# Which MLP units of an HGRN2 + GELU kernel are done by blocks and which by block products: two by blocks instead of three

## The chip, the cores and the metric

The kernel runs on one core of a Trainium2 chip. The metric is the device time of one execution in microseconds, of which three runs of the kernel before are given. The engines have the names of the profile: PE is TensorE (PEld its weight loads), DVE is VectorE, ACT is ScalarE, POOL is GpSimd, and SP is the queue that issues DMAs.

## The reference

The first half is a gated linear recurrence (4 batches, 8 heads, 768 tokens, head dimension 48). The second half is an MLP over the 3072 tokens with a model dimension of 384 and an inner dimension of 2048. The inputs q, k, v and f_logit are float32; the two weight matrices arrive as float64.

```python
def _attn_ref(q, k, v, f_logit):
    f = 1.0 / (1.0 + np.exp(-f_logit))
    state = np.zeros((B, H, D, D))
    for t in range(S):
        state = f[:, :, t, :, None] * state + np.einsum('bhd,bhe->bhde', k[:, :, t], v[:, :, t])
        y[:, :, t] = np.einsum('bhd,bhde->bhe', q[:, :, t], state)
    return y

x = attn_out.transpose(0, 2, 1, 3).reshape(B * S, H * D)

def _moe_ref(x, w_in, w_out):
    h = x @ w_in
    g = h * (1.0 / (1.0 + np.exp(-1.702 * h)))
    return g @ w_out
```

## The kernel before

The 3072 tokens are cut into 12 units of 256, three to a batch. Each unit has an attention (the recurrence in chunks: six levels of scores `sc`, a state `st`, an output `y`, which is turned and written to the tile `xT`) and an MLP (`h` = x times w_in, gelu to `g`, `o` = g times w_out). The attention of unit n is emitted in parts, and between the parts the function `merge` emits pieces of the MLPs of earlier units from the list `fill`, so many columns of TensorE work per part. So TensorE runs the MLP of the earlier units inside the attention of unit n. Attention parts on VectorE are the promotes (L519, L523: X times the decays), the evacuations of scores (L466, L485) and the state (L667, L668); on ScalarE the copies Kc and Qc (L494, L500), which stand between two promotes.

An MLP can be done in two ways.

*Plain, by blocks.* `mlp_h` (L1100) does 16 column blocks of w_in with 3 matmuls of 256 columns each, 48 in all; `mlp_o` (L1114) does 32 matmuls of 384 columns. `mlp_block(n, r)` does a quarter r of the inner dimension, so that it needs only that quarter of the weights; its o is added into a sum by VectorE (L1166). A quarter is usable when its weights are converted from float64 bits (L228 on ScalarE, L230 to L233 on VectorE; 16 pairs of blocks in the order in which the quarters need them, three buffers named `bits`, and a new fetch whenever a pair is done). The argument `pieces` of `merge` says how many conversions its parts carry, and `by` how early.

*By block products.* `mlp_h20` replaces h by 20 products of blocks (4 matmuls of 128 columns each, L1006, 80 in all) that use sums of blocks of w_in (names c1 to c4, p1 to p19) and sums of blocks of x (the tiles E, 12 sums on GpSimd, L968); the products are joined into g by VectorE (L1034) and ScalarE (L1013 to L1036). `mlp_o7` replaces o by 7 products (56 matmuls of 192 columns, L869), with four sums of blocks of w_out (T1 to T4, L783, VectorE) and sums of g (L804 to L813). The order of the 20 products is written out in `WHOLE`; its first seven are c3, c1, p7, a21, c2, p15, p9, and p1 is the tenth.

The sums of w_in are made once. Some need new tiles (`sums_of_w`: c3, p15, c2, p6 and later c1, c4, p12, p4, p16). Others overwrite w_in itself (`sums_in_place`), so they may only run once no plain h needs w_in any more: k, p3, p1 and p14 on GpSimd, p7, p19, p9, p5 and p11 on VectorE. p9 overwrites a11, which p3 reads first. Those with a minus sign, such as p4, run on VectorE (L928), the others of `sums_of_w` on GpSimd (L930); p15's second step reads p4.

Before the change, units 0, 1 and 2 are plain by blocks (`N_FILL` = 3). Unit 3 has a plain h and an o by products. Units 4 to 11 have both by products. The first set of sums of w_in is made inside the attention of unit 3, the second set and those of w_out inside that of unit 4.

TensorE and GpSimd run in the order in which the code emits their work. So do VectorE and ScalarE until `fill_order.close()`; after that, a scheduler may put what is emitted later ahead into gaps that it sees. The tile `xT` has three buffers, which the E tiles share: a unit by products needs all three, so two earlier units' plain h must be over before its sums of x begin.

Of the kernel before, what the change touches and what calls it, by code (L numbers as in the profile page):

```python
# [23 lines left out]
def kernel(  # L24
# [33 lines left out]
    nc = tc.nc  # L58
    B, H, S, D = q.shape
    DM = H * D  # L60
# [4 lines left out]
    U = 256  # L65
# [7 lines left out]
    NK = DM // P  # L73
    NFF = DFF // P
    FG = 4
    PAIRS_AHEAD = 3
    N_FILL = 3
    HALF = U // 2
    SLOT = NP * HALF
    NA = NP * U  # L80
# [236 lines left out]
    last = {}  # L317

    def attention(n):
# [265 lines left out]
        def turn_k(a0):  # L585
            if a0 == 0:
                new_kn()
            if n < N_FILL + 1:
                pt = bank([P, 2, 2, P], f"tkn_{n}_{a0}")
            else:  # L590
                pt = ps.tile([P, 2, 2, P], F32, tag="sc", name=f"tkn_{n}_{a0}")
            for a in range(2):
                for f in range(2):
                    x = (a0 + a) * HALF
                    nc.tensor.transpose(pt[:, a, f, :], slot((KR, KF)[f])[:, x:x + HALF], ident)
            nc.scalar.copy(t["kn"][:, a0:a0 + 2], pt)
# [75 lines left out]
        def _():  # L672
# [45 lines left out]
            xTs[n] = xT  # L718
            if n == 0:
                fetch_weights()  # L720
            if n > N_FILL:
                sums_of_x(n)

        def whole(py):
# [181 lines left out]
    def sums_of_w(names):  # L906

        for name in names:
            if name == "p16":
                WA[name] = wp.tile([P, 2 * DM], F32, tag="s", name="N_p16", bufs=1)[:, :FG * P]  # L910
            else:
                WA[name] = const.tile([P, FG * P], F32, name=f"N_{name}")
        first = (
            ("c3", "a30", "", "a32"), ("p15", "a21", "+", "a31"), ("c2", "a11", "+", "a12"), ("p6", "c2", "+", "a22"),
            ("p6", "p6", "", "c3"),
        )
        second = (
            ("c1", "a01", "+", "a02"), ("c4", "a02", "", "a00"), ("p12", "a11", "", "c4"), ("p4", "c1", "-", "a30"),
            ("p12", "p12", "+", "a10"), ("p16", "a20", "", "a21"), ("p12", "p12", "+", "a20"), ("p15", "p15", "", "p4"),
            ("p16", "p16", "", "a22"),  # L920
        )
        for out, x, op, y in first if "c3" in names else second:
            yield lambda x=(out, x, op, y): sum_of_w(nc.vector if x[2] == "-" else nc.gpsimd, *x)

    def sum_of_w(engine, out, x, op, y):
# [6 lines left out]
    def sums_in_place(engine):  # L932

        assert not w_sums
        if engine == nc.gpsimd:
            for out, at in (("p7", "a01"), ("p19", "a12"), ("p5", "a31"), ("p9", "a11"), ("p11", "a00")):
                WA[out] = WA[at]
            sums = (
                ("k", "a02", "a02", "+", "a30"), ("p3", "a02", "a11", "", "k"), ("p1", "a32", "a21", "+", "c3"),
                ("p14", "a10", "a10", "", "c2"),  # L940
            )
        else:
            sums = (
                ("p7", "a01", "a11", "", "c3"), ("p19", "a12", "c2", "-", "a20"), ("p9", "a11", "c4", "", "a11"),
                ("p5", "a31", "a31", "", "c3"), ("p11", "a00", "a00", "", "c1"),
            )
        for out, at, x, op, y in sums:
            WA[out] = WA[at]
            sum_of_w(engine, out, x, op, y)

    def sums_of_x(n):

# [174 lines left out]
    def mlp_unit(n, fill):  # L1127
# [10 lines left out]
        if width(n) > U:  # L1138
            before = fill[-2 * HF:]
            del fill[-2 * HF:]  # L1140
        if n > N_FILL:
            return mlp_h20(n, g, before) + o
        by_block = {}

        def end():

            g[0], g[1] = (by_block["tile", i] for i in range(2))
            sums_of_a(n, g)
            sums_in_place(nc.gpsimd)
            lanes["o"] = [next(turns) % 4 for _ in range(4)]  # L1150
        return mlp_h(n, range(NFF), by_block) + [(0, end, 0)] + o[:HF] + [(0, lambda: sums_in_place(nc.vector), 0)] + o[HF:]

    sums = {}

# [64 lines left out]
    def merge(n, fill, columns, share, pieces=0, hold=0, by=1.0, chores=[], per=3, deal=()):  # L1219
# [10 lines left out]
        for kind, fn in parts:  # L1230
# [15 lines left out]
            def some(end):  # L1246
                nonlocal done
                while fill and done < end and fill[0][2] <= ready:
                    w, emit, _ = fill.pop(0)
                    emit()  # L1250
                    done += w
            jobs = [convert] * n_ops + chores[:per]
            del chores[:per]
            for i, job in enumerate(jobs):
                some(first + n_columns * i / len(jobs))
                job()
# [13 lines left out]
    def opening():  # L1270
# [44 lines left out]
        for _ in range(NOP):  # L1315
            convert()

    fill = []
    opening()
    fill += mlp_blocks((0, 0)) + mlp_blocks((0, 1))  # L1320
    merge(1, fill, UNIT // 2 - LAG // 2 - 3 * DM, steady, 13, hold=1)
    fill += mlp_blocks((1, 0), (1, 1)) + mlp_blocks((0, 2), (1, 2))
    merge(2, fill, UNIT + 3 * DM, steady, 12)
    fill += mlp_blocks((2, 0), (2, 1)) + mlp_blocks((2, 2), (0, 3)) + mlp_blocks((1, 3), (2, 3))
    w_sums = [*sums_of_w(("c3", "p15", "c2", "p6"))]
    merge(3, fill, 3 * UNIT // 2 - LAG // 2, steady, 5, by=0.7, chores=w_sums, per=1)
    fill_order.close()
    for n in range(N_FILL, NALL):
        fill += mlp_unit(n, fill)
    with nc.allow_non_contiguous_dma("one token"):  # L1330
        for h in range(2):
            nc.sync.dma_start(out=q_end[h * HS:h * HS + D], in_=q[B - 1, h::2, S - 1, :].rearrange("a d -> d a"))
    assert not w_sums
# [38 lines left out]
```

## Time and profile before

| what | value |
|---|---|
| three runs, median (lowest to highest) | 599.36 us (598.73 to 599.51) |
| the profiled execution, first to last instruction | 594.5 us |
| TensorE clock granted over the span | 0.994 of full speed |
| DMA, mean over the span | 98 GB/s |
| plain h, L1100, records and busy time | 384, 89.6 us |
| plain o, L1114 | 192, 65.5 us |
| o by products, L869, TensorE share of the last chain by tile (Y, Z, X, W) | 11%, 8%, 4%, 4% |
| sums of w_in in place on GpSimd begin, after a wait for TensorE's last plain h | 224.3 us |
| first sum of x for a unit by products (unit 4) | 242.5 us |

A line of a timeline reads: start and duration in us, engine, line of the kernel, operation, output and inputs by name, shapes, and how many records were merged into the line; in square brackets stands the time for which the engine was idle before it and what ended the wait. A matmul of float32 leaves two records. A line of a table by stretch has the stretch, its length, the busy time of each engine with its number of records, the clock, and the DMA share and rate.

### The profile page before, as it was taken

What the parts mean: (1) busy time and instruction counts of PE and PEld (TensorE: products, weight loads), DVE (VectorE), ACT (ScalarE), POOL (GpSimd) and SP (SyncE); (2) the same over time, 40 slices, a digit from 0 to 9 for tenths busy, and PEclk for the clock granted to TensorE, in tenths of its full rate; (3) what the DMA queues carried; (4) which work ended last, traced back from release to release, by engine and by line L of the source; (5) the groups of instructions that cost most, each with busy time, mean ns of one, the idle gap of its engine ahead of it and who ended that gap; (6) DMA issues with size and microseconds to landing.
All of it is one profiled execution on the core that took longest, in us unless ns stands there. A gap on an engine that the chain in (4) does not pass through costs nothing.

```text
span 594.5 us, 18457 instructions
## 1 busy us (share of the span) xinstructions
PE 574.9 (97%) x7814; PEld 513.6 (86%) x7814; DVE 429.5 (72%) x696; ACT 291.9 (49%) x613; POOL 138.4 (23%) x214
## 2 busy tenths in 40 slices
PE   6879899999999999999999999999999999999997
PEld 6756776867768789999999999999999999999897
DVE  2898987964866858789778778786887786462284
ACT  4746643453334353474474474573663564452440
POOL 4031200230027216610610700800700602203000
PEclk9979999999999999999999999999999999999999
DMA  7947859840243552353552343553361211001000
GB/s 181 215 124 179 193 145 225 217 100 1 52 106 66 145 130 65 80 139 77 127 146 51 84 113 91 130 134 60 88 168 44 63 38 29 28 3 27 28 1 27
DMA packets 82834, 58.29 MB, mean 98 GB/s; under 512 B 33153, under 2 KB 74785, under 8 KB 82753
## 3 DMA queue, kind: packets, MB, share of 16 engines
q1 hardware_dynamic: 82416, 56.73, 38.9%
q8 instruction: 61, 1.00, 0.7%
q10 hardware_dynamic: 337, 0.39, 0.3%
q14 instruction: 20, 0.16, 0.1%
HBM read 43.98 MB, written 8.39 MB: 88 GB/s over the span
## 4 chain that ended last, share of the span: by engine, by line
PE 87%; DVE 7%; ACT 3%; issue 1%; DMA 1%; POOL 1%; SPq 0%; DVEq 0%; ACTq 0%
PE h L1006 17%; PE h L1100 13%; PE o_Y L869 11%; PE o L1114 10%; PE o_Z L869 8%; PE h_y L1006 6%; PE sc L425 6%; PE o_X L869 4%; PE o_W L869 4%; PE y L689 2%; PE t L357 2%; PE y L534 2%; PE sc L643 1%; DVE X L519 1%; ACT yT L703 1%
## 5 line engine op out<-in xcount | busy, mean ns | idle before, releaser
L1100 PE MATMUL h<-xT,w_in 128*128 128x256 f32 x384 | 89.6, 388 | 1.4 <-DMA xT<-yT 1.4
L523 DVE TENSOR_TENSOR X<-X,tot 128x1024 f32<-128x1024 f32 x45 | 57.0, 1266 | 39.8 <-PE sc L425 33.2
L1100 PEld LDWEIGHTS h<-xT,w_in 128*128 128x128 f32 x384 | 72.8, 193 | 13.8 <-DMA xT<-yT 2.4
L494 ACT COPY Kc<-X 128x512 f32<-128x512 f32 x72 | 48.4, 672 | 65.7 <-DVE X L523 51.5
L1114 PE MATMUL o<-w_out,g 128*128 128x384 f32 x192 | 65.5, 491 | 0.4 <-DVE w_out L233 0.4
L968 POOL TENSOR_TENSOR E<-xT 128x128 f32<-128x128 f32 (+1 forms) x32 | 17.9, 571 | 204.0 <-DMA xT<-yT 112.0
L1114 PEld LDWEIGHTS o<-w_out,g 128*128 128x128 f32 x192 | 35.4, 190 | 22.8 <-DVE w_out L233 1.0
L1006 PE MATMUL h<-E,w_in 128*128 128x128 f32 (+1 forms) x420 | 53.4, 275 | 0.0
L869 PE MATMUL o_Y<-T,S 128*128 128x192 f32 x288 | 50.6, 329 | 0.0
L1006 PEld LDWEIGHTS h<-E,w_in 128*128 128x128 f32 x420 | 50.1, 192 | 0.0
L1036 ACT ACTIVATE g<-g 128x512 f32<-128x512 f32 (+1 forms) x63 | 35.6, 584 | 26.0 <-DVE g L1034 25.3
L1104 ACT ACTIVATE g<-h 128x256 f32<-128x256 f32 x64 | 23.8, 382 | 49.0 <-PE h L1100 48.6
L869 PEld LDWEIGHTS o_Y<-T,S 128*128 128x128 f32 x288 | 46.8, 190 | 0.5
L1034 DVE TENSOR_TENSOR g<-g,h 128x512 f32<-128x512 f32 (+1 forms) x52 | 31.8, 632 | 14.3 <-PE h L1006 13.3
L485 DVE COPY_PREDICATED A<-masks,sc 128x256 f32<-128x256 uint32 (+1 forms) x98 | 42.0, 506 | 0.1
L703 ACT COPY yT<-y 48x256 f32<-48x256 f32 x88 | 32.2, 366 | 18.3 <-PE y L689 17.2
L372 POOL TENSOR_SCALAR F<-F 128x1024 f32<-128x1024 f32 x10 | 17.2, 1716 | 95.9 <-ACT F L375 84.3
L345 DVE STREAM_TRANSPOSE X<-raw 128x512 f32<-128x512 f32 x36 | 38.1, 1105 | 0.1
L425 PEld LDWEIGHTS sc<-X,Kc 48*64 48x64 f32 x1440 | 26.2, 136 | 11.1 <-ACT Kc L494 4.8
L425 PE MATMUL sc<-X,Kc 48*64 48x64 f32 x1440 | 31.0, 222 | 4.8 <-ACT Kc L494 1.9
L1034 DVE TENSOR_TENSOR g<-g,h_y 128x512 f32<-128x512 f32 (+1 forms) x26 | 16.5, 634 | 22.3 <-PE h_y L1006 21.4
L1025 ACT ACTIVATE g<-h 128x512 f32<-128x512 f32 (+1 forms) x46 | 26.1, 576 | 10.8 <-PE h L1006 10.6
(162 smaller groups left out, 1156.2 us busy)
## 6 DMA issues: line engine op xcount, KB each, us to landing
bits<-in_moe_w_out_dram SPq DMA_DIRECT2D x8, 768.0 KB, 7.2
raw<-in_f_logit_dram SPq DMA_DIRECT2D x48, 96.0 KB, 3.5
raw<-in_k_dram SPq DMA_DIRECT2D x48, 96.0 KB, 3.0
bits<-in_moe_w_in_dram SPq DMA_DIRECT2D x8, 576.0 KB
raw<-in_q_dram SPq DMA_DIRECT2D x44, 96.0 KB, 2.3
k_tok<-z SPq DMA_DIRECT2D x56, 64.0 KB, 1.8
kt<-k_tok SPq DMA_DIRECT2D x14, 256.0 KB, 2.8
out_dram<-osb SPq DMA_DIRECT2D x18, 192.0 KB, 2.7
```

The lines of the kernel that those rows point to most:

```text
L345: nc.vector.transpose(view(out, at, [[HALF, NP], [step, R4], [R4 * step, 32]]), by_half[:, j, f].rearrange("p a (j d) -> p (a j) d", j=R4) ...
L425: nc.tensor.matmul(t["sc"][h][g * HS:(g + 1) * HS, a, s, :], lhsT=t["Kc", l][rows(h), x:x + HS], rhs=rhs(h, a, g), start=True, stop=True,)
L485: moved = nc.vector.copy_predicated(out=view(A, c * HALF + at, dims), mask=mask.bitcast(U32), data=got)
L494: nc.scalar.copy(c.rearrange("p (n two m) -> p n two m", two=2, m=m), view(X, KF * SLOT, [[2 * m, SLOT // (2 * m)], [(KR - KF) * SLOT + m, ...
L523: nc.vector.tensor_tensor(x, x, y, ALU.mult)
L703: nc.scalar.copy(view(yT[rows(h)], at, [[U, NP], [step, HS]]), py[columns(h, g), g, :, f, :])
L869: nc.tensor.matmul(t[name], lhsT=lhs(f), rhs=rhs(f), start=(new and i == 0), stop=(i == HF - 1), skip_group_check=True,)
L1006: nc.tensor.matmul(ph[:, t], lhsT=WA[a][:, f * P:(f + 1) * P], rhs=E[n][b], start=(root and t == 0), stop=not goes_on, skip_group_check=True,)
L1034: nc.vector.tensor_tensor(to, to, part, ALU.add if sign > 0 else ALU.subtract)
L1036: nc.scalar.activation(to, to, AF.Gelu_apprx_sigmoid)
L1100: nc.tensor.matmul(ph, lhsT=w_in[:, c, ff * P:(ff + 1) * P], rhs=xTs[n][:, c, :], start=(c == 0), stop=(c == NK - 1))
L1114: nc.tensor.matmul(t["po"], lhsT=g[ff // FG][:, ff % FG, tt * P:(tt + 1) * P], rhs=w_out[:, ff, :], start=(ff == ffs[0]), stop=(ff == ffs[ ...
```

## The change

Units 0 and 1 stay plain by blocks. Unit 2 becomes a unit by products whole, and so does unit 3 (its h; its o was already). `merge` for unit 3 now emits the last quarters of units 0 and 1 and then unit 2 by products. All sums of w_in are made inside unit 3's attention: twelve of them as chores of `merge`, whatever is left of them together with unit 2's sums of x and the sums in place after the first o matmul of the last blocks. p9 and the two steps of p16 come after the last o of these blocks, and there the program order of VectorE and ScalarE ends. The eight sums of w_out are put among unit 2's products. Two conversion instructions move from the attention of unit 3 into that of unit 2, and those that stay come earlier in it. `turn_k` of unit 3 uses the bank `sc` for its transposes.

```diff
+    N_BLOCK = 2
...
-            if n < N_FILL + 1:
+            if n < N_FILL:
                 pt = bank([P, 2, 2, P], f"tkn_{n}_{a0}")
...
-            if n > N_FILL:
+            if n >= N_FILL:
                 sums_of_x(n)
...
-            ("p12", "p12", "+", "a10"), ("p16", "a20", "", "a21"), ("p12", "p12", "+", "a20"), ("p15", "p15", "", "p4"),
-            ("p16", "p16", "", "a22"),
+            ("p12", "p12", "+", "a10"), ("p12", "p12", "+", "a20"), ("p15", "p15", "", "p4"),
         )
-        for out, x, op, y in first if "c3" in names else second:
+        last = ("p16", "a20", "", "a21"), ("p16", "p16", "", "a22")
+        for out, x, op, y in {"c3": first, "c1": second, "p16": last}[names[0]]:
...
-        if n > N_FILL:
-            return mlp_h20(n, g, before) + o
-        by_block = {}
-
-        def end():
-
-            g[0], g[1] = (by_block["tile", i] for i in range(2))
-            sums_of_a(n, g)
-            sums_in_place(nc.gpsimd)
-            lanes["o"] = [next(turns) % 4 for _ in range(4)]
-        return mlp_h(n, range(NFF), by_block) + [(0, end, 0)] + o[:HF] + [(0, lambda: sums_in_place(nc.vector), 0)] + o[HF:]
+        return mlp_h20(n, g, before) + o
...
-            jobs = [convert] * n_ops + chores[:per]
-            del chores[:per]
+            jobs = [convert] * n_ops + [lambda: chores and chores.pop(0)()] * per
...
+    def last_blocks():
+
+        hs, os = zip(*(mlp_block(n, NGR - 1) for n in range(N_BLOCK)))
+
+        def sums_left():
+            for x in w_sums:
+                x()
+            w_sums.clear()
+            sums_of_x(N_BLOCK)
+            sums_in_place(nc.gpsimd)
+            last_w.extend(sums_in_place(nc.vector))
+            for x in last_w[:-1]:
+                x()
+            lanes["o"] = [next(turns) % 4 for _ in range(4)]
+
+        def order_ends():
+            last_w[-1]()
+            for x in sums_of_w(("p16",)):
+                x()
+            fill_order.close()
+        o = sum(os, [])
+        return sum(hs, []) + o[:1] + [(0, sums_left, 0)] + o[1:] + [(0, order_ends, 0)]
+
+    def first_whole(n):
+
+        h, of_b = mlp_unit(n, fill), [*sums_of_b()]
+        while of_b:
+            x = of_b.pop()
+            h.insert(2 * len(of_b) + 4, (0, x, 0))
+        return h
...
-    merge(2, fill, UNIT + 3 * DM, steady, 12)
-    fill += mlp_blocks((2, 0), (2, 1)) + mlp_blocks((2, 2), (0, 3)) + mlp_blocks((1, 3), (2, 3))
-    w_sums = [*sums_of_w(("c3", "p15", "c2", "p6"))]
-    merge(3, fill, 3 * UNIT // 2 - LAG // 2, steady, 5, by=0.7, chores=w_sums, per=1)
-    fill_order.close()
+    merge(2, fill, UNIT + 3 * DM, steady, 13)
+    fill += last_blocks() + first_whole(N_BLOCK)
+    w_sums = [*sums_of_w(("c3", "p15", "c2", "p6")), *sums_of_w(("c1", "c4", "p12", "p4"))]
+    last_w = []
+    merge(3, fill, 2 * UNIT + H20 + 7 * HF * HC - LAG - (3 * UNIT // 2 - LAG // 2), steady, 4, by=0.3, chores=w_sums, per=2)
...
-    of_b = [*sums_of_b()]
-    for x in sums_of_w(("c1", "c4", "p12", "p4", "p16")):
-        w_sums += of_b[:1] + [x]
-        del of_b[:1]
-    w_sums += of_b
     for n in range(4, NALL):
-        merge(n, fill, (H20 if n > N_FILL + 1 else NFF * NK * U) + 7 * HF * HC, late, chores=w_sums if n == 4 else [])
+        merge(n, fill, H20 + 7 * HF * HC, late)
```

More of the change, by code (lines that the diff above doesn't have):

```diff
@@ L943, in sums_in_place @@
             sums = (
-                ("p7", "a01", "a11", "", "c3"), ("p19", "a12", "c2", "-", "a20"), ("p9", "a11", "c4", "", "a11"),
-                ("p5", "a31", "a31", "", "c3"), ("p11", "a00", "a00", "", "c1"),
+                ("p7", "a01", "a11", "", "c3"), ("p19", "a12", "c2", "-", "a20"), ("p5", "a31", "a31", "", "c3"),
+                ("p11", "a00", "a00", "", "c1"), ("p9", "a11", "c4", "", "a11"),
             )
@@ L948, in sums_in_place @@
             WA[out] = WA[at]
-            sum_of_w(engine, out, x, op, y)
+            if engine == nc.gpsimd:
+                sum_of_w(engine, out, x, op, y)
+        return [lambda x=(out, x, op, y): sum_of_w(engine, *x) for out, at, x, op, y in sums]
     def sums_of_x(n):
@@ L1332 @@
             nc.sync.dma_start(out=q_end[h * HS:h * HS + D], in_=q[B - 1, h::2, S - 1, :].rearrange("a d -> d a"))
-    assert not w_sums
-    of_b = [*sums_of_b()]
-    for x in sums_of_w(("c1", "c4", "p12", "p4", "p16")):
-        w_sums += of_b[:1] + [x]
-        del of_b[:1]
-    w_sums += of_b
     for n in range(4, NALL):
-        merge(n, fill, (H20 if n > N_FILL + 1 else NFF * NK * U) + 7 * HF * HC, late, chores=w_sums if n == 4 else [])
+        merge(n, fill, H20 + 7 * HF * HC, late)
     for _, emit, _ in fill:
```

## The prediction

> **What bounds the kernel now.** I read the page's busy shares and slices first: TensorE (PE) is full.
>
> ```profile
> PE 574.9 (97%) x7814; PEld 513.6 (86%) x7814; DVE 429.5 (72%) x696; ACT 291.9 (49%) x613; POOL 138.4 (23%) x214
> ...
> PE   6879899999999999999999999999999999999997
> ...
> DVE  2898987964866858789778778786887786462284
> ...
> POOL 4031200230027216610610700800700602203000
> ```
>
> Then the table of waits, TensorE alone, 40 to 240 us. It sums to under 4 us in 200, so TensorE's work sets the end, and work taken off it is time won unless a new wait takes its place.
>
> ```profile
> PE tkn L595 <- DVE X L519: 1.6, 1, 1.6
> PE sc L425 <- DVE st L668: 0.5, 2, 0.3
> PE y L689 <- DVE st L668: 0.5, 1, 0.5
> ```
>
> Then busy time by stretch (columns: PE, PEld, DVE, ACT, POOL). From 124 to 150 us, which the change refills, VectorE (DVE) idles 4.5 and 7.4 us and GpSimd (POOL) nearly throughout. The last row is one steady unit: 43.20 us, all TensorE.
>
> ```profile
> 124.00:137.60 13.60, 13.60 (x124) 9.92 (x117) 9.14 (x12) 5.27 (x12) 0.82 (x1) 1.00 0.22 50
> 137.60:150.30 12.70, 12.70 (x106) 8.72 (x100) 5.28 (x10) 3.83 (x9) 0.00 (x0) 1.00 0.01 1
> ...
> 286.40:329.60 43.20, 43.20 (x657) 42.00 (x658) 32.65 (x52) 23.98 (x47) 11.86 (x19) 1.00 0.45 108
> ```
>
> **What comes off TensorE.** Durations are start to start in the timeline; a matmul leaves two records.
>
> ```profile
> 170.49 5.38 PE L1114 MATMUL o<-w_out,g 128*128 128x384 f32 x16
> 175.71 1.46 PE L1100 MATMUL h<-xT,w_in 128*128 128x256 f32 x6
> ...
> 205.78 18.40 PE L1100 MATMUL h<-xT,w_in 128*128 128x256 f32 x84
> 224.01 2.11 PE L869 MATMUL o_Y<-w_out,g 128*128 128x192 f32 x12
> ...
> 236.70 2.76 PE L869 MATMUL o_Y<-T,S 128*128 128x192 f32 x16
> 239.30 2.76 PE L869 MATMUL o_Z<-T,g 128*128 128x192 f32 x16
> ```
>
> Plain o: 5.22 us for 8, 0.653 each. Plain h: 18.23 for 42, 0.434. o by products: 2.60 for 8, 0.325. h by products (255.04 to 256.82, 16 records): 0.2225. A unit's h falls from 48 x 0.434 = 20.83 to 80 x 0.2225 = 17.80: 3.03 less, for units 2 and 3, 6.06. Unit 2's o falls from 32 x 0.653 = 20.90 to 56 x 0.325 = 18.20: 2.70. Sum: **-8.76 us**. Cross-check: unit 4's attention with unit 3's h took 46.3 us (187.9 to 234.2), a steady unit 43.2; the 3.1 is one unit's h.
>
> **What is added, and hidden.** Units 2 and 3 now each need 12 GpSimd sums of x (0.42 us each) and ten VectorE sums of g (0.69), ScalarE's copies too. The built order of TensorE, VectorE and ScalarE is unchanged over its last 300 rows, and unit 3's is that of a steady unit, which hides all this behind 43.2 us of TensorE: nothing. Unit 2's sums of g stand behind p9 (below) as a steady unit's stand behind its scores. Two conversion instructions move from the third merge into the second (1.9 us of VectorE); its waits of 1.92, 1.23 and 0.38 at 98.7, 101.5 and 107.6 cover them; without these, up to 1.9. The last weight fetch moves ahead on SP's queue, stores of sums give way to stores of osb, and q_end's small load moves back: TensorE waited 0.3 us for DMAs from 40 to 240 us, so nothing. Unit 3's turn_k takes the sc bank, idle then: nothing.
>
> **The new chain.** The last blocks' h come earlier, unit 0's at 130.7 us instead of 159, unit 1's at 137 instead of 176, and unit 2's products follow. VectorE's order up to them is one queue. I lay it on the old clock.
>
> Up to 130.5 us it is the old schedule; two sums for T (1.82) and two F transposes (1.95) fit gaps of 1.58 and 2.16. Then conversion of pair 14 (2.7), three sums (1.4), two for T (1.8): 136.4. TensorE gives scores at 136.5; two promotes with the ScalarE copy between, and evacuation, take 5.45 (138.73 to 144.17 in the old trace): 141.95. Pair 15 (2.8): 144.75. TensorE wants that pair at its third o: 130.7 + 12 h 5.2 + scores 1.1 + 12 h 5.2 + scores 1.1 + two o 1.3 = 144.6. No slack.
>
> Then promote 1.15, evacuation 0.65, N_p4 0.6: 147.15. GpSimd waits for N_p4: p15 1.24, 12 sums of x 5.0, k and p3 2.5: 155.9. VectorE: four in-place sums 2.6, four o sums 1.9, transposes 1.95, three for T 2.75: 156.35, then p9 0.65: 157.0. TensorE's seventh product needs p9: 144.6 + 14 x 0.653 + 6 x 0.89 = 159.1. Slack 2.1. Behind p15 on GpSimd stand all sums of x and in place; behind p9 on VectorE T4's second half and unit 2's sums of g, for which ScalarE's gelus and then unit 2's o wait, all later than the seventh product.
>
> **The price not in that sum.** GpSimd now runs ten weight sums without a break from 120.1, where it ran three, and VectorE works beside it throughout. The timeline shows what happens when both add in SBUF:
>
> ```profile
> 123.54 1.27 POOL L930 TENSOR_TENSOR N_c<-w_in 128x512 f32<-128x512 f32 x1
> ...
> 224.26 3.19 POOL L930 TENSOR_TENSOR w_in<-w_in 128x512 f32<-128x512 f32 x2 [14.39 <-PE h L1100]
> ```
> ```profile
> 120.73 1.72 DVE L523 TENSOR_TENSOR X<-X,F 128x1024 f32<-128x1024 f32 x1 [1.58 <-ACT Qc L500]
> ...
> 138.73 1.23 DVE L523 TENSOR_TENSOR X<-X,tot 128x1024 f32<-128x1024 f32 x1 [3.23 <-PE sc L425]
> ...
> 224.65 1.67 DVE L806 TENSOR_TENSOR g<-g,g 128x512 f32<-128x512 f32 x1
> ...
> 227.49 1.74 DVE L930 TENSOR_TENSOR w_in<-N_c,w_in 128x512 f32<-128x512 f32 x1 [1.17 <-POOL w_in L930]
> ```
>
> Alone, L523 takes 1.23 and a 128x512 sum 0.69. Eight collisions cost VectorE 0.49, 0.80, 0.28 (L523), 1.05, 0.98, 1.05, 1.07 (sums) and 0.40 (L230): mean 0.77. GpSimd loses too (3.19 for two). Transposes and PSUM readers did not lose.
>
> First part, up to pair 15: eleven VectorE instructions on SBUF alone meet those sums, 11 x 0.77 = 8.4 at most. Counting only kinds seen waiting (three L523, two tensor_scalar), 3.8; no collision, 0.15. GpSimd's five small products at 71.8 took 4.03 beside L232 and L233, against 2.07 at 118.1, so the conversions do collide; but some sums will fall into transposes and evacuations. I take six, 4.6. Second part, to p9: GpSimd waits behind four in-place sums (2.6), VectorE in front of T, T, T and p9 (4 x 0.77 = 3.1): 5.7 - 2.1 slack = 3.6 at most; seen kinds only, 2.6 + 0.77 - 2.1 = 1.3; none, 0. I take 1.7, nearer the row. Stall: 6.3, between 0.15 and 12.0. A gain here is excluded: TensorE cannot run before its operands.
>
> The Trainium skill (SBUF — State Buffer, section "SBUF: two separate sides") speaks against this change: it calls the port pair that VectorE and GpSimd share an exclusive lock, held for the whole instruction, against any Vector instruction with two SBUF inputs. By that rule every one of these instructions waits, and the sum would lie at the upper end, near 602.6; by the kinds seen waiting it is 595.7. The waits above (0.28 to 1.07 of a 1.24 us sum) fit a lock met midway.
>
> **Sum.** -8.76 + 6.3 = -2.46 on a span of 594.5, so 592.0. About 4.9 us lie around the span (median 599.36), unchanged: **596.9 us**. From unit 4's first scores on, nothing changes but the clock's offset, so a stall is never won back.
>
> **Rivals.** (1) The cover holds: GpSimd's sums fall into VectorE's transposes and waits, stall 0.15, time 590.8. For it: 124 to 150 us has 12 us of idle VectorE. Against: the queue laid out above fills them. (2) All given back: stall 7.6 to 10.0, 598.2 to 600.6, no change. For it: most of the fifteen collisions at 0.77. (3) Slower: TensorE stands at the seventh product because p9 is last in a chain through both engines (N_p4, p15, twelve sums of x, k, p3, p9). All fifteen collisions: 8.4 + 3.6 = 12.0, time 602.6; it decides from where p9 lands later than 159.1 + 8.76 + 1.2 = 169.1 on the old clock. For it: 3.19 and 1.67 at 224 us show strict turns. Against: it needs every collision. That the change does not do what it says is out: the built order has units 2 and 3 in 80 and 56 products.
>
> **Numbers.** What this kernel's measurement tells from no change is 0.2%, 1.2 us. Forecast (part of the gain kept, 592 to 598): 0.41. Rival 1: 0.17. Rival 2: 0.18. Rival 3: 0.24. Faster 0.58, same 0.18, slower 0.24. Range 591.0 to 602.0: from rival 1 to most of rival 3; the forecast's own is 592 to 598.
>
> **What would show it.** TensorE's plain h records fall from 384 to 192, plain o from 192 to 128. In its waits a new row of some microseconds: the third matmul of the last blocks' o or their scores behind w_out's conversion or X (part one), and an h product behind w_in (p9, part two). GpSimd's ten sums take clearly over 12.4 us from start to end, and N_p4 starts near 151, not 147. If there is no such wait, rival 1 is right; if the wait is on a DMA or on E, the chain I named is wrong; if TensorE's steady units are longer than 43.2 us, the cover I took for nothing is gone.

## The result and the profile after

| what | before | after |
|---|---|---|
| median on the same chip, 20 runs each | 598.80 us (597.21 to 600.51) | 600.86 us (599.28 to 602.30) |
| ratio, 95% interval | | 1.0036 (1.0026 to 1.0047) |
| profiled execution's span | 594.5 us | 600.0 us |

The change made the kernel slower by 0.36%, 2.06 us. The profiled execution is the slower one by 5.5 us; why it shows more than the medians is said below.

From the profile's page after: busy time by engine, three of the rows of slices, and the shares of the last chain.

```profile
PE 573.4 (96%) x7990; PEld 522.5 (87%) x7990; DVE 449.3 (75%) x721; ACT 300.8 (50%) x620; POOL 155.6 (26%) x238
...
PE   7969899898889999999999999999999999999997
...
DVE  2797994989978878779778789767877786462284
...
POOL 3031020076480440430420610700700701303000
...
PE 75%; DVE 14%; DMA 4%; ACT 3%; SPq 2%; issue 2%; DVEq 0%; ACTq 0%
```

The row of TensorE now has an 8 from 105 to 120 us and from 135 to 180 us, where it was full (a slice is 15 us). In the last chain VectorE has risen from 7% to 14% and TensorE has fallen from 87% to 75%. The plain h records are 192 and the plain o records 128, so the work has moved as meant. From the table of TensorE's waits after, 40 to 240 us (total, times, longest):

```profile
PE h L1103 <- DVE sum L1159: 2.1, 3, 1.2
PE h L1009 <- DVE sum L1159: 2.1, 2, 1.6
...
PE sc L426 <- DVE A L486: 1.4, 1, 1.4
PE tkn L596 <- DVE sum L1159: 1.2, 1, 1.2
PE o L1117 <- DVE w_out L234: 1.2, 2, 0.8
```

L1159 is VectorE's sum of o of the blocks; it frees the bank (one of four, which h, o and unit 2's transposes tkn share with others) into which TensorE's next product goes. Of the rows left out, the largest is 1.7 us for the DMA of xT, at 41.5 us, where the code is still the same. No row names p9 (L931).

To see where the time went I read four marks on TensorE's timeline: unit 2's first scores at 71 to 74 us (A, the code up to there is the same in all kernels), unit 3's first, with which the last blocks' stretch begins (B, 123.74 before, 129.76 after; sc_23 in the expectations), unit 3's last (C, sc_25), and unit 4's first (D, sc_27, 187.89 and 196.49).

| stretch (us) | before | after | difference |
|---|---|---|---|
| start to A | 71.02 | 74.01 | +2.99 |
| A to B | 52.72 | 55.75 | +3.03 |
| B to D | 64.15 | 66.73 | +2.58 |
| D to end | 406.61 | 403.51 | -3.10 |

I take the first line for chance: in the fourteen executions profiled for this study A lies anywhere from 70.48 to 74.01, with the same code ahead of it. Without it the profile says +2.5, near the medians' 2.06. A to B also scatters: in this and the four runs below that leave its code nearly alone it is 54.75 to 56.29, so that its loss is 2.0 to 3.6. The last line is unit 3's h, foretold at 3.03. Of the 8.76 us taken off TensorE 5.73 lie between B and D. TensorE was busy through all of this stretch before (64.15 of 64.15 us), so that it would have taken 58.42 us without a stall. It took 8.31 more (6.16 of them idle; the rest lies in rows that take longer when they follow a wait), and A to B lost 3.03.

**A to B.** VectorE after, then before, then ScalarE, the SP queue and TensorE after:

```profile
105.16 0.56 DVE L231 TENSOR_SCALAR s<-a 128x768 int32<-128x768 int32 x1 [5.56 <-ACT a L229]
105.63 1.28 DVE L520 TENSOR_TENSOR X<-X,tot 128x512 f32<-128x512 f32 x2
```
```profile
101.51 0.56 DVE L230 TENSOR_SCALAR s<-a 128x768 int32<-128x768 int32 x1 [1.23 <-ACT a L228]
```
```profile
104.22 0.90 ACT L229 ACTIVATE a<-bits 128x768 f32<-128x768 f32 x1 [7.61 <-DMA bits<-in_moe_w_out_dram]
```
```profile
94.22 4.97 SPq L279 DMA_DIRECT2D raw<-in_k_dram  x8
99.31 0.39 SPq L211 DMA_DIRECT2D bits<-in_moe_w_out_dram  x1
```
```profile
109.89 1.56 PE L1103 MATMUL h<-xT,w_in 128*128 128x256 f32 x6 [0.51 <-DVE sum L1159]
112.67 0.66 PE L596 MATMUL tkn<-ident,X 128*128 128x128 f32 x4 [1.22 <-DVE sum L1159]
```

Read backwards: the fetch of pair 11's bits is issued at 99.31, behind unit 3's raw loads; ScalarE waits 7.61 us for it; VectorE's first conversion instruction of pair 11 waits 5.56 us for ScalarE. Before, this instruction stood behind the two promotes (L519), and waited 1.23. Moved one step earlier, it holds up the promotes, the rest of the conversion and the sums of o behind them (at 109.29 and 112.09). TensorE did not wait for the promotes; it waited for the banks that these two sums free.

**B to D.** VectorE after, in the stretch in which GpSimd makes its ten weight sums (128.87 to 145.5, 16.6 us):

```profile
133.86 2.29 DVE L524 TENSOR_TENSOR X<-X,tot 128x1024 f32<-128x1024 f32 x1 [1.26 <-ACT Qc L501]
...
137.92 1.03 DVE L231 TENSOR_SCALAR s<-a 128x768 int32<-128x768 int32 x1
138.87 0.54 DVE L1159 TENSOR_TENSOR sum<-sum,o 128x384 f32<-128x384 f32 x1
139.33 1.16 DVE L232 TENSOR_SCALAR a<-s 128x768 int32<-128x768 int32 x1
140.41 0.54 DVE L1159 TENSOR_TENSOR sum<-sum,o 128x384 f32<-128x384 f32 x1
140.88 1.56 DVE L233 SCALAR_TENSOR_TENSOR a<-bits,a 128x768 f32<-128x768 uint32 x1
142.36 0.54 DVE L1159 TENSOR_TENSOR sum<-sum,o 128x384 f32<-128x384 f32 x1
142.83 1.55 DVE L234 TENSOR_TENSOR w_out<-a,s 128x768 f32<-128x768 f32 x1
144.30 2.03 DVE L784 TENSOR_TENSOR T<-w_out,T 128x768 f32<-128x768 f32 x1
```

Alone the six that are no sums of o take 1.23, 0.56, 0.56, 0.96, 0.95 and 0.95: they lose 4.4 us. (A seventh, the promote at 131.33, took 1.27; there GpSimd's sum was the longer one, 2.39 us where one takes 1.24.) The sums of o, which read PSUM, lose nothing themselves (0.54), but stand behind the others. TensorE's h waits for them, and the scores that end the stretch for the mask after the late promotes:

```profile
139.46 3.11 PE L1103 MATMUL h<-xT,w_in 128*128 128x256 f32 x12 [1.23 <-DVE sum L1159]
142.96 1.56 PE L1103 MATMUL h<-xT,w_in 128*128 128x256 f32 x6 [0.39 <-DVE sum L1159]
...
152.42 0.69 PE L426 MATMUL sc<-Qc,Kc 48*64 48x64 f32 x32 [1.43 <-DVE A L486]
...
169.23 2.05 PE L1009 MATMUL h<-E,w_in 128*128 128x128 f32 x16 [1.59 <-DVE sum L1159]
...
172.01 1.06 PE L1009 MATMUL h<-xT,N_p 128*128 128x128 f32 x8
173.10 2.02 PE L1009 MATMUL h<-E,w_in 128*128 128x128 f32 x16
```

The third product (169.23) waits 1.59 us for the bank of the last o, whose sum stands behind three sums of T. The seventh, p9's, starts at 173.10, 1.09 us after the sixth, where a product takes 0.89: p9 costs 0.2 us. VectorE's rows for both:

```profile
165.38 1.07 DVE L784 TENSOR_TENSOR T<-w_out,T 128x768 f32<-128x768 f32 x1
166.37 2.33 DVE L784 TENSOR_TENSOR T<-w_out 128x768 f32<-128x768 f32 x2
168.63 0.54 DVE L1159 TENSOR_TENSOR sum<-sum,o 128x384 f32<-128x384 f32 x1
171.22 1.74 DVE L931 TENSOR_TENSOR w_in<-N_c,w_in 128x512 f32<-128x512 f32 x1 [2.04 <-POOL w_in L931]
```

### The profile page after: what moved, and what is told of

Its sections match the earlier page's. It is cut to its first block, busy times and chain, and to the rows that moved or that the text cites. A ratio compares the mean times of both kernels' runs of the same rounds, so it can differ in the third digit from the quotient of the medians.

```text
span 600.0 us, 18902 instructions
## 1 busy us (share of the span) xinstructions
PE 573.4 (96%) x7990; PEld 522.5 (87%) x7990; DVE 449.3 (75%) x721; ACT 300.8 (50%) x620; POOL 155.6 (26%) x238
## 3 DMA queue, kind: packets, MB, share of 16 engines
q8 instruction: 63, 1.03, 0.8%
## 4 chain that ended last, share of the span: by engine, by line
PE 75%; DVE 14%; DMA 4%; ACT 3%; SPq 2%; issue 2%; DVEq 0%; ACTq 0%
PE h L1009 20%; PE o_Y L870 13%; PE o_Z L870 9%; PE h_y L1009 8%; PE sc L426 5%; PE o_X L870 5%; PE o_W L870 5%; DMA bits<-in_moe_w_in_dram 2%; PE h L1103 2%; PE y L690 2%; PE y L535 2%; DVE X L524 1%; PE sc L644 1%; DVE A L486 1%; DVE a L233 1%
## 5 line engine op out<-in xcount | busy, mean ns | idle before, releaser
L1009 PE MATMUL h<-E,w_in 128*128 128x128 f32 (+1 forms) x532 | 67.7, 275 | 1.6 <-DVE sum L1159 1.6
L1009 PEld LDWEIGHTS h<-E,w_in 128*128 128x128 f32 x532 | 63.4, 192 | 2.0 <-DVE sum L1159 1.8
L1039 ACT ACTIVATE g<-g 128x512 f32<-128x512 f32 (+1 forms) x77 | 44.4, 595 | 31.9 <-DVE g L1037 31.2
L1103 PE MATMUL h<-xT,w_in 128*128 128x256 f32 x192 | 48.1, 401 | 3.9 <-DVE sum L1159 2.1
L1037 DVE TENSOR_TENSOR g<-g,h 128x512 f32<-128x512 f32 (+1 forms) x64 | 39.6, 641 | 15.0 <-PE h L1009 13.9
L1103 PEld LDWEIGHTS h<-xT,w_in 128*128 128x128 f32 x192 | 36.8, 199 | 11.7 <-DVE sum L1159 3.7
L1117 PE MATMUL o<-w_out,g 128*128 128x384 f32 x128 | 44.0, 493 | 1.2 <-DVE w_out L234 1.2
L1117 PEld LDWEIGHTS o<-w_out,g 128*128 128x128 f32 x128 | 23.5, 190 | 16.6 <-DVE w_out L234 1.9
L1009 PE MATMUL h<-E,N_c 128*128 128x128 f32 (+1 forms) x236 | 32.4, 279 | 0.5 <-DVE sum L1159 0.5
L417 POOL TENSOR_TENSOR tot<-F 128x512 f32<-128x512 f32 x12 | 12.5, 1040 | 72.1 <-DVE st L668 65.8
```

The costliest lines, as they stand in the source:

```text
L1009: nc.tensor.matmul(ph[:, t], lhsT=WA[a][:, f * P:(f + 1) * P], rhs=E[n][b], start=(root and t == 0), stop=not goes_on, skip_group_check=True,)
L1037: nc.vector.tensor_tensor(to, to, part, ALU.add if sign > 0 else ALU.subtract)
L1039: nc.scalar.activation(to, to, AF.Gelu_apprx_sigmoid)
L1103: nc.tensor.matmul(ph, lhsT=w_in[:, c, ff * P:(ff + 1) * P], rhs=xTs[n][:, c, :], start=(c == 0), stop=(c == NK - 1))
L1117: nc.tensor.matmul(t["po"], lhsT=g[ff // FG][:, ff % FG, tt * P:(tt + 1) * P], rhs=w_out[:, ff, :], start=(ff == ffs[0]), stop=(ff == ffs[ ...
```

## The experiments

My theory after this reading: 3.0 us are the late fetch, and 8.3 us are VectorE's queue, stretched by GpSimd, in front of what frees TensorE's banks and scores. The rivals were that VectorE simply has too much work, and that GpSimd's chain to p9 binds, as the prediction's slower case has it. All twelve runs are listed here first. Ratios are to the kernel before, run on the same chip; A to D are the marks above, read in one profiled execution each.

| run | median us | ratio (95%) | A to B | B to C | C to D |
|---|---|---|---|---|---|
| the change | 600.86 | 1.0036 (1.0026 to 1.0047) | 55.75 | 22.66 | 44.07 |
| 1 conversions undone | 603.13 | 1.0075 (1.0053 to 1.0096) | 52.73 | 28.58 | 43.03 |
| 2 fetch first | 598.70 | 0.9996 (0.9982 to 1.0009) | 53.56 | 22.66 | 44.40 |
| 3 one deal | 607.97 | 1.0159 (1.0140 to 1.0178) | 56.11 | 27.20 | 48.09 |
| 4 small sums | 594.66 | 0.9930 (0.9907 to 0.9952) | 56.29 | 18.81 | 42.76 |
| 5 p9 apart | 599.44 | 1.0022 (1.0008 to 1.0035) | 54.82 | 22.61 | 43.55 |
| 6 T late | 612.32 | 1.0239 (1.0213 to 1.0264) | 54.75 | 21.22 | 57.75 |
| 7 fetch first, early sums | 597.06 | 0.9986 (0.9972 to 0.9999) | 54.58 | 18.80 | 46.16 |
| 8 as 7, T late | 608.07 | 1.0163 (1.0137 to 1.0189) | 54.54 | 18.91 | 55.86 |
| 9 as 7, N_p4 early | 600.36 | 1.0033 (1.0017 to 1.0049) | 54.56 | 20.10 | 47.70 |
| 10 as 9, p9 apart | 601.41 | 1.0060 (1.0042 to 1.0079) | 54.55 | 20.09 | 49.59 |
| 11 conversions undone, early sums | 602.93 | 1.0066 (1.0041 to 1.0091) | 53.56 | 24.35 | 47.65 |
| 12 as 7, N_p4 late | 595.35 | 0.9951 (0.9933 to 0.9969) | 54.55 | 18.81 | 44.36 |

D to the end is 403.4 to 404.0 us in all of them.

### 1. The conversions put back

```diff
-    merge(2, fill, UNIT + 3 * DM, steady, 13)
+    merge(2, fill, UNIT + 3 * DM, steady, 12)
-    merge(3, ..., steady, 4, by=0.3, chores=w_sums, per=2)
+    merge(3, ..., steady, 5, by=0.3, chores=w_sums, per=2)
```

> Only the moved conversions are undone (12 instructions in the second merge, 5 in the third). My theory now: of what the change gave back, 3.0 us were lost near 105 us, because pair 11's first conversion stood ahead of two promotes in VectorE's order and waited 5.56 us for a Prelude that waited for its weight fetch. Then the 5.56 us wait is gone, the stretch from the first scores to sc_23 is 3 us shorter, and the time falls from 600.9 to about 597.9 (0.9985 of the kernel before). Rival A: the extra conversion work on VectorE merely moves into the chain of the last blocks, which is as long as before in absolute terms, so the 3 us come back there: 600.9 (1.0036). Rival B: the extra conversion delays pair 15 by its own 1 to 1.9 us: 599 to 600.

The wait of 5.56 us went (1.15 in its place) and A to B fell by 3.02, as expected. But the time rose by 2.3 us: B to C took 5.92 us more. Rival A's direction holds, and twice its size. With two conversion instructions more in the stretch, a promote on VectorE begins only at 142.51, ScalarE's copy Kc waits 8.31 us for it, and the gelus stand behind that copy. TensorE in this run:

```profile
141.16 4.15 PE L1103 MATMUL h<-xT,w_in 128*128 128x256 f32 x18 [2.43 <-DVE sum L1159]
149.50 4.54 PE L1103 MATMUL h<-xT,w_in 128*128 128x256 f32 x12 [4.18 <-ACT g L1107]
```

So the two moved instructions are a gain within the change: 3 us lost, 6 us saved.

### 2. The fetch ahead of the raw loads

```diff
-    parts[1] = parts[1][0], lambda: (second(), [load_raw(n + 1, j) for j in range(3)])
+    third = parts[2][1]
+    parts[1] = parts[1][0], lambda: (second(), load_raw(n + 1, 0))
+    parts[2] = parts[2][0], lambda: (third(), [load_raw(n + 1, j) for j in (1, 2)])
```

> The 13 and 4 conversions of the changed kernel stay; only unit 3's raw loads of q and k are issued one part later, so that pair 11's weight fetch stands ahead of those loads on SP's queue. If the 3.0 us near 105 us are the fetch's lateness, the 5.56 us wait of VectorE shrinks under 1.5 us and the time falls to about 598 (0.9987); as VectorE then has no conversion more in the last blocks, it may be a little below the run that undoes the conversions. Rival: the loss there is VectorE having no room for two conversions more (1.9 us of work), not the wait on the fetch: the wait goes but the time stays within 1 us of 600.9.

Measured 598.70, 2.2 us less than the change, and level with the kernel before. The SP queue issues pair 11's fetch at 82.37 where it did at 99.31. VectorE's next wait is a smaller one, for the fetch after that:

```profile
97.22 0.56 DVE L231 TENSOR_SCALAR s<-a 128x768 int32<-128x768 int32 x1
...
106.96 0.56 DVE L231 TENSOR_SCALAR s<-a 128x768 int32<-128x768 int32 x1 [1.78 <-ACT a L229]
```

Of the 3.03 us that A to B lost, 2.19 were the fetch; the work of the two conversions is all still there. 0.84 us stay against the kernel before (53.56 against 52.72), and TensorE has one new wait there, 0.45 us at 118.48 for VectorE's state.

### 3. All weight sums dealt at once

```diff
-    merge(3, ..., by=0.3, chores=w_sums, per=2)
+    merge(3, ..., by=0.3, chores=w_sums, per=11)
```

> Only the deal of the eleven weight sums is changed (all in one part), which moves VectorE's N_p4 from behind sc_25's masks to behind unit 1's second sum of o, some 13 us earlier; GpSimd's order is unchanged. My theory: GpSimd's 12.75 us wait for N_p4 stands in the chain that ends at p9 and at the sums of x; with it gone, the sums of x land by about 157 and p9 by about 165 on the profile's clock, the waits of 1.59 us (third product) and about 2 us (seventh product) go, and the time falls by 3 to 4 us to about 597.4 (0.9977). Rival: the chain is bound by collisions and by VectorE's own queue, which the sums of x now meet in the conversion of the last pair: no gain or under 1 us, 600 to 601.

7 us slower than the change: the expectation fell, and the rival, which has the cause, was far too small (600 to 601). N_p4 ran at 143.19 (157.50 in the change) and GpSimd's wait for it shrank from 12.75 to 0.63 us. The sums of x then waited for TensorE's h, whose buffers they take. They and the sums in place met VectorE's conversion and sums in place: VectorE's four sums in place, 4.0 us in the change (158.10 to 162.11), took 6.4 from 160.97 on, and the sums of o behind them came late. The first product waited 4.07 us for such a sum. This run also put two conversion instructions ahead of two sums of o (B to C 4.5 us longer), so it tests two things at once; runs 9 and 12 separate them.

### 4. GpSimd's weight sums made small

```diff
-            engine.tensor_tensor(WA[out], WA[x], WA[y], ALU.add if op else ALU.subtract)
+            engine.tensor_tensor(*(WA[i][:, :16 if engine == nc.gpsimd else FG * P] for i in (out, x, y)), ALU.add if op else ALU.subtract)
```

GpSimd's sums, those in place included, leave out all but 16 of 512 columns; the new operands are set to zero by GpSimd beforehand.

> GpSimd's weight sums are done on 16 of 512 columns (the rest of these operands is zero or unsummed, so the output is not the reference's); the order of all engines is unchanged. This takes away the collisions with VectorE and GpSimd's time in the chain, not VectorE's own work. My theory: of the 8.2 us lost between sc_23 and sc_27, 6 to 8 are the collisions and GpSimd's chain: 593 to 595 (0.990 to 0.994), with VectorE's conversions and T sums near 140 us back at their lone durations of 0.56 to 0.96. Rival: the loss is VectorE's own queue (two conversions, T sums and promotes in one order): at most 2 us less, 599 to 600.9.

594.66, 6.2 us under the change, as expected. The table by stretch (length, then PE, PEld, DVE, ACT and POOL busy), first the change from B to the middle scores and on to C, then this run:

```profile
129.76:144.45 14.69, 13.08 (x107) 8.69 (x107) 13.40 (x16) 6.34 (x13) 14.30 (x10) 1.00 0.40 99
144.45:152.42 7.97, 6.54 (x90) 5.54 (x89) 6.68 (x10) 2.91 (x8) 1.06 (x1) 1.00 0.01 2
```
```profile
129.62:141.90 12.28, 12.28 (x107) 8.92 (x106) 10.95 (x17) 6.33 (x13) 5.87 (x17) 1.00 0.51 122
141.90:148.43 6.53, 6.53 (x90) 5.54 (x89) 4.72 (x9) 2.92 (x7) 0.00 (x0) 1.00 0.01 3
```

TensorE is busy throughout, and VectorE's time for the same work falls by 4.4 us over the two rows. B to C has no stall left: the 3.85 us there are GpSimd's weight sums and nothing else. C to D keeps 42.76 - 39.61 = 3.15 of its 4.46 us (39.61 is 58.42 less the 18.81 of B to C). TensorE's waits left there are 0.77 us for pair 15's conversion, as in the change, 1.27 at the third product for the sum of o behind three sums of T, and 0.25 at y.

### 5. p9 in an operand of its own

```diff
-            ("p12", "p12", "+", "a10"), ("p12", "p12", "+", "a20"), ("p15", "p15", "", "p4"),
+            ("p12", "p12", "+", "a10"), ("p9", "c4", "", "a11"), ("p12", "p12", "+", "a20"), ("p15", "p15", "", "p4"),
...
-                ("p11", "a00", "a00", "", "c1"), ("p9", "a11", "c4", "", "a11"),
+                ("p11", "a00", "a00", "", "c1"),
```

> The changed kernel, but p9 gets an operand of its own instead of being made in place, so it no longer waits for k and p3 on GpSimd, nor stands last in VectorE's order; nothing else moves. The prediction's slower rival named p9 as the operand that holds TensorE. My theory now: it does not. In the changed kernel the seventh product starts 1.09 us after the sixth where a product takes 0.89, so p9 costs 0.2 us; what holds TensorE is o's banks, freed by VectorE's sums (L1159) that stand in its queue behind colliding work. Then the time stays within 0.5 us of the changed kernel's, 600.4 to 601 (1.0027 to 1.0040). Rival (p9 is last in the chain): 2 us or more are won, at most 598.9 (1.000).

599.44 lies between the two cases. B to D fell by 0.57 us; the seventh product starts 0.89 us after the sixth. The median fell by 1.4 us, by 0.8 in ratio to the kernel before (the two ratios' intervals overlap). The chain to p9 is worth half a microsecond, not the stall.

### 6. T's sums behind p9

```diff
         def order_ends():
             ...
-            fill_order.close()
...
-        return h
+        return h + [(0, fill_order.close, 0)]
```

> The changed kernel, but VectorE's seven sums of w_out for T (L784) no longer stand in program order ahead of p9: two of them leave the stretch before sc_23, two the stretch before sc_25, three the stretch before the last blocks' last sum of o, 6.9 us of VectorE in all; they go between unit 2's sums of g. If the bound is VectorE's queue as such (any work in front of the promotes and o sums), 3 to 4 us are won: 597 to 598 (0.997 to 0.9987). If only the collisions with GpSimd bind, under 1 us: 600 to 600.9. If unit 2's products need VectorE's sums of g earlier than T lets them, it is slower than the changed kernel, over 601.5.

The third case, and further than it said: 612.32. B to C gained 1.4 us, but now T's sums hold up the sums of g that free the banks of unit 2's products, and its g altogether. The first sum of g runs at 176.09, behind three of T's sums and four transposes; TensorE waits until 176.87 (the row names no releaser; that sum of g ended at 176.77) and again until 195.00:

```profile
PE y L535 <- DVE g L1037: 5.9, 1, 5.9
PE h_y L1009 <- issue: 5.2, 1, 5.2
```

So the program order must end early, as in the change. What T's sums alone cost at their early place this run does not show: it keeps the transposes and all other work on VectorE and ScalarE in program order through unit 2's products too.

### 7. The fetch first, and seven weight sums early

```diff
-                    parts.insert(i - 3, ("B", begin_f))
+                    parts.insert(i - 3, ("B", lambda: ([x() for x in sums_of_w(("c3", "p15", "c2", "p6", "p12"))], begin_f())))
...
-            ("c1", "a01", "+", "a02"), ("c4", "a02", "", "a00"), ("p12", "a11", "", "c4"), ("p4", "c1", "-", "a30"),
-            ("p12", "p12", "+", "a10"), ("p12", "p12", "+", "a20"), ("p15", "p15", "", "p4"),
+            ("c1", "a01", "+", "a02"), ("c4", "a02", "", "a00"), ("p12", "p12", "", "c4"), ("p4", "c1", "-", "a30"),
+            ("p15", "p15", "", "p4"),
```

p12's first two steps, now a11 + a10 + a20, move up with c3, c2 and p6.

> As the run that issues pair 11's weight fetch ahead of the raw loads of q and k (598.7), and seven of GpSimd's ten weight sums, those that need no part of the last w_in group, are put ahead of unit 3's F, where GpSimd stood idle from 79 to 113 us; only c1, c4, p12's last step and p15's stay in the last blocks. If the collisions are the price of the stretch from sc_23 to sc_27 (5.2 us there went when the sums were cut to 16 columns), most of it goes: that stretch falls from 67.1 to about 62 and the time to 594 to 595.5 (0.992 to 0.9945), below the kernel before. Rival: the sums collide with VectorE's conversions and promotes of unit 2 near 95 to 108 us instead, which TensorE waits for too, and what is won later is lost there: 597.5 to 599.

597.06: faster than the change and just below the kernel before (the interval ends at 0.9999), but between the two cases. B to C fell to 18.80, the same as with the small sums. C to D rose by 1.76 over run 2's and A to B by 1.0, where two promotes now met GpSimd's sums (3.44 for two at 95.51, against 1.29 for two at 89.47, where GpSimd was idle) and a sum of o later freed its bank 0.73 late. In the new order VectorE's N_p4 stands ahead of the last promote and its masks, not behind them as in the change. So GpSimd's chain began earlier, and its sums in place fell on T's sums; the sum of o behind them, which the third product waits for, came later:

```profile
159.04 3.14 DVE L784 TENSOR_TENSOR T<-w_out 128x768 f32<-128x768 f32 x2
```
```profile
162.70 3.50 PE L1009 MATMUL h<-E,w_in 128*128 128x128 f32 x16 [2.41 <-DVE sum L1159]
```

### 8. All three together

This is run 7 with run 6's edit.

> The early weight fetch, the early weight sums and T's sums behind p9, all three. If the three prices are separate (fetch 2.2 us, collisions 5.2 us, T's sums in VectorE's queue up to 3 us), the stretch from sc_23 to sc_27 comes near the 58.5 us that TensorE's work alone takes, and the time is 591.5 to 593.5 (0.988 to 0.991). Rival: T's sums and the collisions are one price (one queue on VectorE), so that it is no better than the run with the early sums alone: 594 to 595.5.

608.07; neither case. B to C kept run 7's gain, and C to D most of run 6's loss (55.86 against 57.75).

### 9 and 10. N_p4 earlier still; and p9 apart as well

```diff
-    merge(3, ..., by=0.3, chores=w_sums, per=2)
+    merge(3, ..., by=0.3, chores=w_sums, per=4)
```

> The run with early fetch and early weight sums (597.06), and VectorE's N_p4 moved from behind the last conversion (148.8 us there) to behind unit 1's first sum of o (near 138), where GpSimd idled 18.9 us for it; the last block sum of unit 1 moves behind one conversion instruction. Then p15 and the first half of the sums of x are done before sc_25, and VectorE's last sums of T and in place no longer meet them: the wait of 2.4 us at the third product falls to about 1 and the pause of 1.5 us behind it goes: 594 to 595.5 (0.993 to 0.9955). Rival: the sums of x now collide with promotes and the last conversion from 139 to 149 and delay sc_25 or the third o by as much: 596.5 to 599.

> As the run just described, and p9 in an operand of its own behind the last conversion on VectorE. If p9 costs as little as in the changed kernel (0.8 us or less by the run on it), this one stands within 0.8 us of its neighbour without it. If p9, which in the run with early sums ended at 165.1 for a product at 168.0, is now last, it would win more than 1 us.

Run 9 took 3.3 us more than run 7, 1.3 of it before C (one sum of o stands behind a conversion there) and 1.5 after: the rival's cause is right, its price too small (596.5 to 599). N_p4 at 138.72 sets off GpSimd at 139.49, and the two engines then take turns all the way. Two of VectorE's sums in place, 1.80 in the change, take 3.42, and the first product waits for the sum of o behind them. VectorE and TensorE in this run:

```profile
157.14 3.42 DVE L931 TENSOR_TENSOR w_in<-w_in,N_c 128x512 f32<-128x512 f32 x2
160.49 1.00 DVE L1159 TENSOR_TENSOR sum<-sum,o 128x384 f32<-128x384 f32 x2
```
```profile
164.83 3.43 PE L1009 MATMUL h<-E,N_c 128*128 128x128 f32 x16 [3.82 <-DVE sum L1159]
```

Run 10 shows again that p9 is not what is late: with p9 apart, one sum more stands in front of the sums of o, and the wait is 4.60. Its time rose by 1.05 us, a little more than the 0.8 allowed for.

### 11. The conversions put back, with early sums

This is run 1's edit with run 7's early sums, without the early fetch.

> The conversions back at 12 and 5 and the early weight sums, without the early fetch. Undoing the conversions alone took away the 5.56 us wait and yet was 2 us slower than the changed kernel: from sc_23 on it lost 4.9 us more. If those 4.9 us are the two conversions more standing among GpSimd's collisions and in front of the sums of o, they shrink to the conversions' own 1.9 us or less once the sums are early: 595.5 to 598 (0.995 to 0.999), level with the run that has the early fetch and the early sums (597.06). If they are VectorE's load itself, whatever GpSimd does: 600 or more.

602.93: my expectation fell; the other case's range (600 or more) holds. B to C took 24.35, against 28.58 in run 1 and 18.80 in run 7. So four of run 1's ten excess microseconds there are collisions, and the rest I put down to the order on VectorE itself: pair 13 is now converted inside the stretch, c1 and c4 wait 12.14 us for it and so still collide, and the gelu behind Kc still costs TensorE 2.50. What B to C gained over run 1, C to D lost (47.65 against 43.03): the third product waited 3.30 us for a sum of o behind three of T's sums.

### 12. N_p4 back behind the masks

```diff
-    merge(3, ..., by=0.3, chores=w_sums, per=2)
+    merge(3, ..., by=0.3, chores=w_sums, per=1)
```

The only thing that this moves against run 7 is VectorE's N_p4, behind the last promote and its masks.

> The run with the early fetch and the early weight sums (597.06, 0.9986), with one thing changed: VectorE's N_p4 stands behind sc_25's masks again, as in the changed kernel, two instructions later. GpSimd's p15, sums of x and sums in place then begin some 2 us later against VectorE's queue. My theory: GpSimd's wait for N_p4 keeps the two engines apart, so a later start costs nothing and takes collisions away from VectorE's sums in place and T's sums: the stretch from sc_25 to sc_27 goes back from 46.2 us to the 44.1 to 44.4 it had with N_p4 in that place, and the time falls to 595 to 596 (0.9945 to 0.996). Rival: an earlier N_p4 is what the products need (GpSimd's chain binds): the later one costs its 2 us, 598 to 599.5.

595.35, as expected, and the best of all with whole sums: 0.9951 of the kernel before, 0.9933 to 0.9969. C to D fell to 44.36. GpSimd, VectorE and TensorE in this run: the first row is to be compared with the wait of 12.75 us in the change, the next three, which are as short in run 7, with the durations shown for the change, and the last two with run 7's:

```profile
151.85 1.65 POOL L931 TENSOR_TENSOR N_p<-N_p,N_p 128x512 f32<-128x512 f32 x1 [20.74 <-DVE N_p L929]
```
```profile
134.22 0.57 DVE L231 TENSOR_SCALAR s<-a 128x768 int32<-128x768 int32 x1
...
136.11 0.94 DVE L233 SCALAR_TENSOR_TENSOR a<-bits,a 128x768 f32<-128x768 uint32 x1
...
138.31 0.95 DVE L784 TENSOR_TENSOR T<-w_out,T 128x768 f32<-128x768 f32 x1
...
159.97 2.33 DVE L784 TENSOR_TENSOR T<-w_out 128x768 f32<-128x768 f32 x2
```
```profile
162.82 2.05 PE L1009 MATMUL h<-E,w_in 128*128 128x128 f32 x16 [1.60 <-DVE sum L1159]
```

While GpSimd idles for 20.74 us VectorE runs at full speed, and TensorE needs VectorE.

## Why the prediction was wrong in its sign

- *The 8.76 us taken off TensorE*: right. D to the end is 3.10 us shorter, where 3.03 were foretold; in run 4 the stretch B to C holds TensorE's work without a gap. The rest of the 5.73 between B and D lies under stalls and was not measured alone.
- *Steady units and the clock's offset after unit 4's first scores*: right. D to the end is the same in all variants, and a stall was never won back.
- *Two conversion instructions at nothing, covered by waits of 1.92, 1.23 and 0.38; SP's queue at nothing*: these are the first steps that failed. Their price is 3.0 us (2.0 to 3.6 over the profiles), more than the 1.9 given as the bound without cover. The step took the waits of VectorE as free room. The one of 1.23 was itself a wait for pair 11's bits, so an instruction moved ahead of it does not fill it but takes it along, with promotes and sums of o behind it. Run 2 shows that the fetch is the cause of 2.2 of the 3.0; the other 0.8 went only where the conversions were put back as well (run 1). "TensorE waited 0.3 us for DMAs" was true and no argument: the DMA was two engines away from TensorE.
- *Part one of the collisions, 4.6 us*: right in size, in part by luck: six out of eleven was a choice, and six lost, 4.4 us in all, of which 3.85 reached TensorE. Wrong was the place. It was not pair 15 at the third o (0.77 there in the change, and as much in run 4 without collisions), but the banks that sums of o free, and a mask.
- *Part two, 1.7 us (0 to 3.6)*: mis-sized, 4.46 measured, so that the stall was 11.3 in all, not 6.3. The step laid out VectorE's queue up to p9 and asked when p9 lands. The sums of o in the same queue were counted as work, not as what the first and third products wait for (0.48 and 1.59 us). Another 0.77 is the wait for pair 15 at the third o, which the prediction had in its first part. p9 itself cost 0.2 us in the profile, about 0.6 by run 5.
- *What would show it*: N_p4 "near 151" ran at 157.50, less 6.02 of offset 151.5; GpSimd's ten sums took 16.6 us, over 12.4. The wait named for p9 is not there.
- *About 4.9 us around the span*: misread, without effect on the difference. A run's time is 1.7 us over its span in the change (601.73 for 600.0) and 2.1 in the kernel before (596.5 for 594.4, in a later run); so the execution of the kernel before that was profiled (594.5) was a quick one.
- *The rivals*: the time lies just above the second (598.2 to 600.6). The third had the sign, but its mechanism did not decide: p9 landed at 166.9 on the old clock, under its 169.1.
- *The Trainium skill's lock* (SBUF — State Buffer, "SBUF: two separate sides") agrees with these rows. With both engines adding in SBUF, six instructions of VectorE lost 0.47 to 1.08 us each. Two of the six are TENSOR_SCALARs, with one tile as input. The page puts a second class under the lock, instructions in a 2-port performance mode; no row names a mode, but 0.56 us for 768 elements against 0.95 for a two-input sum of as many fits one. The sums of o, with one input in PSUM, lost nothing, as the page would have it. Taken for every instruction it put the time at 602.6, nearer to 600.86 than the forecast, but through a term that it overstated: the first part's six were enough.

In sum: -8.76 + 3.03 + 3.85 + 4.46 = +2.6 in the profile without its late start; +2.06 in the medians.

Of C to D's remaining 3.15 us, run 4 shows waits of 1.27 behind T's sums and 0.77 for pair 15; what the sums in place, earlier in the same queue, add to either was not separated. Sums placed behind F instead of ahead of it, which might save the 1.0 us that the early ones cost in A to B, were not tried.

## What to carry to other kernels

An idle wait is free room only if what ends it would not also hold up the moved instruction: follow it to its own cause, through the second engine and the DMA queue, before an edit is costed at nothing. In an in-order queue, ask of every instruction behind the stretched ones what it releases; here it was TensorE's banks, not the operand at the queue's end. And where two engines slow each other, making one start earlier can cost more than its idling: keep VectorE's critical stretch clear, and move the other's work to where VectorE is not waited for.

## What the runs showed of the hardware

- The same code took from 70.48 to 74.01 us to reach the same scores in fourteen profiled executions. In that of the change (74.01) TensorE's granted clock from 30 to 45 us was 0.58, in that of the kernel before (71.02) 0.77. A single span can mislead by 3 us on a change of 2.
- Beside GpSimd's ten sums six of seven VectorE promotes, conversions and sums on SBUF alone took 9.6 us for 5.2 of lone work, and the ten sums 16.6 for 12.4. VectorE's TENSOR_SCALARs, which read one tile, lost too: 1.03 and 1.16 instead of 0.56. Sums that read one operand from PSUM ran untouched between them.
